# Two batches' heads in the opening of a fused attention and mixing kernel

## The chip, the cores and the metric

One core of a Trainium2 chip runs the kernel. The metric is device time in microseconds of that core. The time before is 978.15 us, the median of three runs (977.51 to 978.64).

## The reference, cut to what matters

```python
# q, k, v: (8, 8, 576, 64), float32
scores = 1 / sqrt(64) * q @ k.T
mask_local   = (rel >= 0) & (rel < 32)                       # heads 0..3, rel = i - j
mask_strided = (rel >= 0) & (j % 32 == i % 32)               # heads 4..7
attn = softmax(where(mask, scores, -1e9))
x = (attn @ v) as (8, 576, 512)
h = x^T @ U @ V                                              # along the sequence, rank 32
u = x + h^T
out = u + relu(u @ w_ch1) @ w_ch2                            # 512 -> 2048 -> 512
```

U, V, w_ch1 and w_ch2 arrive as float64. Every float32 product of the large GEMMs is made of three: high part by high part, high by low, low by high.

## The kernel before, in words

**Tiling.** The 8 x 576 rows are nine blocks of 512: block n < 8 holds the first 512 rows of batch n, block 8 the last 64 rows of all batches. For each block the two GEMMs run over 16 chunks of 128 hidden features (`fc`). A step is `gemm1(fc)` (12 matmuls 128x512, L616), a relu split into a high part `gh` on ScalarE (L620) and a low part `gl` on VectorE (L621), and `gemm2` of the chunk before (12 matmuls, L633). The GEMMs read u transposed, as `uh` and `ul`, which `split` makes from `raw` at a block's end (L607, L608).

**Weights.** A chunk of both weights is 1 MB of 64-bit words. `load_weights` brings it in on SP's queue, `weights` converts it: one ScalarE instruction (L122), three of VectorE (L124, L125, L127), a rounding on ScalarE (L173) and a difference on VectorE (L174). The buffer `cv` in which this is done is double and lies in the one "wide" buffer, which the strided heads need afterwards. `N_FIRST` chunks are converted ahead of the first step, in halves of 512 columns; the others one chunk a step in block 0, each made to follow in order the `gl` of the step `BEHIND` = 5 before it.

**Attention.** Heads come in pairs; below, "a head" is such a pair of 128 columns. The first `NSP` = 2 batches run local and strided heads alike through `early_pair`: `scores` (L301, L307), `probabilities` (max L316, difference L317, exp L321), `transposed` (L328, copy L331), `outputs` (PV, L341), `normalised` (L350, L351, L353, L357). Then comes the head's quarter of u^T: x is transposed on PE (L277) and multiplied with U (L238, L240), copied and split into `tst` (L245 to L247), and multiplied with V onto the same sums (L249); for batch 0 the result goes into `uh` and `ul` (L259, L260), for batch 1 into `raw` (L255). Strided heads of these batches are computed with rows sorted by class and go through DRAM (`od`) into natural order, on POOL's queue (L99). From batch 2 on, strided heads are element by element on POOL and VectorE (`strided_heads`, L400, L402, L428, L430), copied in place by ScalarE (L445, L449), and local heads go through PE.

**Order.** `first_attention` is the opening: all of batch 0's heads, staggered by one stage. Then `convert(2 * N_FIRST)`, then the steps. After each half step (a slot, 32 to a block) `advance` pulls items of the next batch's attention so that they are spread from slot `a0` to `a1` of the block; what is left at `a1` is drained there. In block 0 that is batch 1: tail of batch 0, then its four heads. In block 1 it is batch 2. Strided heads are spread separately, from slot 20 of block 0 on and not before all chunks are converted; where the attention of a batch says "strided" they are drained. A planner orders the instructions of each engine by its own cost model with this order as priority; `issue_after` adds an order on one engine.

**Buffers.** PSUM has two pairs of banks named acc, one px and two single banks ph. In the opening all three pairs rotate; in the steps acc belongs to gemm2 and px alone to attention. The tag "att" has five SBUF buffers for s_sb, PT, x, tmp, s_st and others; in the opening a ring of slices of weight buffers stands in for it. Weight buffers `w8` to `w15` hold batch 0's head data as `late`, `w7` is `early`. The tag "half" has three.

Of the kernel before, what the change touches and what calls it, by code (L numbers as in the profile page):

```python
# [7 lines left out]
F32 = mybir.dt.float32  # L8
F32R = mybir.dt.float32r
# [6 lines left out]
NEG = -1.0e9  # L16
ATT_BUFS = 5
NSP = 2
N_EARLY = 19
N_LATE = 48  # L20
N_STRIDED = 66
LAG = 1
LAGB = 3
CLA = 5
N_FIRST = 7
BEHIND = 5
A_EARLY = (1, 24, N_EARLY)
A_SECOND = (1, 28, 50)
A_LATE = (1, 28, N_LATE)
A_TAIL = (4, 20, 8)  # L30
S0 = {b: 32 * (b - 1) - 12 for b in range(2, 8)}
# [6 lines left out]
def fused_kernel(ctx, tc, pairs, strided, U, V, w_in, masks, eye, out):  # L38
# [21 lines left out]
    def att(shape, name, dtype=F32):  # L60
        if ring:
            s = ring.pop(0)
            ring.append(s)
            n = 1
            for x in shape[1:]:
                n *= x
            s = s[0:shape[0], 0:n]
            return s if len(shape) == 2 else s.rearrange("p (t h x) -> p t h x", t=shape[1], h=shape[2]) if len(shape) == 4 \
                else s.rearrange("p (t x) -> p t x", t=shape[1])
        return ap_.tile(shape, dtype, name=name, tag="att", bufs=ATT_BUFS)  # L70

    def half_buffer(width, name):
        return ap_.tile([128, 1176], F32, name=name, tag="half", bufs=3)[:, 0:width]
# [86 lines left out]
    def weights():  # L160
        cvs = wide_buffer("cv")
        for fc in range(NFC):
            load_ahead(fc + 1)
            cv = cvs[:, 1152 * (fc % 2):1152 * (fc % 2) + 1024]
            n = 512 if fc < N_FIRST else 1024
            with tc.issue_after(marks["gl"][fc - BEHIND]) if fc >= N_FIRST else nullcontext():
                for x in range(0, 1024, n):
                    to_f32(raws[fc][:, x:x + n], cv[:, x:x + n], 128, n)
            fv = cv.rearrange("p (i x) -> p i x", i=2)
            yield  # L170
            parts = w_parts[fc] = const.tile([128, 2, 2, 512], F32R, name=f"w{fc}", tag=f"w{fc}")
            for x in range(2) if fc < N_FIRST else [slice(0, 2)]:
                nc.scalar.copy(out=parts[:, x, 0], in_=fv[:, x])  # L173
                nc.vector.tensor_tensor(out=parts[:, x, 1], in0=fv[:, x], in1=parts[:, x, 0].bitcast(F32), op=ALU.subtract)  # L174
            yield
# [10 lines left out]
    halves = [slice(64 * hh, 64 * hh + 64) for hh in range(2)]  # L186

    def load_qk(b, pr):
        qk = late[2 * ORDER0.index(pr)][:, 0:2 * S] if b == 0 else half_buffer(2 * S, "qk")
        dma(out=qk, in_=pair_source(b, pr)[:, 0:2 * S])  # L190
        return qk[:, 0:S], qk[:, S:2 * S]

    def load_v(b, pr):
        vx = late[2 * ORDER0.index(pr) + 1][:, 0:PAIR - 2 * S] if b == 0 else half_buffer(PAIR - 2 * S, "v")
        dma(out=vx, in_=pair_source(b, pr)[:, 2 * S:PAIR])
        return vx.rearrange("p (c x) -> p c x", x=D + 1)

# [3 lines left out]
    def early_pair(b, pr, od, last):  # L201

        tb = 64 * (b % 2)
        by_class = pr >= 2
        kT, qT = load_qk(b, pr)
        yield
        if b == 0:
            vt = load_v(b, pr)
            yield
        with tc.issue_after(marks["PV"][3]) if b else nullcontext():  # L210
            sp = scores(kT, qT, mask_s if by_class else mask_l)
        s_sb = yield from probabilities(sp)
        if b:
            vt = load_v(b, pr)
        yield
        PT = transposed(s_sb)
        yield
        op = outputs(PT, vt)
        cs = slice(2 * pr * D, 2 * pr * D + 2 * D)
        if by_class:  # L220
            x = att([128, 640], "x").rearrange("p (t x) -> p t x", t=5) if b else \
                early[:, 320 + 640 * (pr - 2):960 + 640 * (pr - 2)].rearrange("p (t x) -> p t x", t=5)
            main, last_x, Um = x[:, 0:4, :], x[0:64, 4, :], U_c
            normalised(op, x)
        else:
            xg, xt = x_tiles(b)
            main, last_x, Um = xg[:, :, cs], xt[tb:tb + 64, cs], U_sb
            normalised(op, main, last_x, tb)
        p0 = 0 if by_class else tb
        yield  # L230
        pu = psx2().rearrange("p a x -> p (a x)")
        pm = ps_h.tile([128, 512], F32, name="ph")[0:32, 0:128] if b == 0 else pu[0:32, 640:768]
        lead = x_transposed(pu, [main[:, t, :] for t in range(4)])
        if by_class:
            lead = x_transposed(pu[:, 512:576], [last_x])
        with tc.issue_after(lead):
            for t in range(4):
                nc.tensor.matmul(pm, Um[:, t, :], main[:, t, :], start=t == 0 and not (b and by_class), stop=False,  # L238
                                 skip_group_check=True, tile_position=(0, 0))
            nc.tensor.matmul(pm, Um[p0:p0 + 64, 4, :], last_x, start=False, stop=True, skip_group_check=True,  # L240
                             tile_position=(p0, 0))
        if b not in tsts:
            tsts[b] = ap_.tile([96, DM], F32R, name="tst")
        tst = tsts[b]
        nc.scalar.copy(out=tst[0:32, cs], in_=pm)  # L245
        nc.scalar.copy(out=tst[64:96, cs], in_=pm)
        nc.vector.tensor_tensor(out=tst[32:64, cs], in0=pm, in1=tst[0:32, cs].bitcast(F32), op=ALU.subtract)  # L247
        for c0, n, Vm in ((0, 512, Vc), (512, 64, Vc_last)) if by_class else ((0, 512, Vst),):
            nc.tensor.matmul(pu[:, c0:c0 + n], tst[:, cs], Vm[:, 0:n], start=False, stop=True, skip_group_check=True)  # L249
        src = pu[:, 0:512]  # L250
        if by_class:
            src = pu[:, 0:S].rearrange("p (c j) -> p j c", j=NCH)[:, 0:16, :]
        if b:
            dst = raw[:, :, :, pr, :]
            nc.scalar.copy(out=dst, in_=src.rearrange("p (s a) x -> p s a x", s=4) if by_class else  # L255
                           src.rearrange("p (s a x) -> p s a x", s=4, a=4))
        else:
            hi, lo = (u[:, pr, :].rearrange("p (j c) -> p j c", c=32) if by_class else u[:, pr, :] for u in (uh, ul))
            one = nc.scalar.copy(out=hi, in_=src)  # L259
            two = nc.vector.tensor_tensor(out=lo, in0=src, in1=hi.bitcast(F32), op=ALU.subtract)  # L260
            marks["split0"] = (two.ins, one.ins)
        if by_class:
            oc = 2 * pr * D - 4 * D
            far_dma(out=od[0:512, oc:oc + 2 * D].rearrange("(t p) d -> p t d", p=128), in_=main)
            far_dma(out=od[512:576, oc:oc + 2 * D], in_=last_x)
        yield
        if last:
            od_reads(b, od)

    def x_transposed(pu, parts):  # L270

# [255 lines left out]
    def first_attention():  # L527
        tsts[0] = ap_.tile([96, DM], F32R, name="tst")
        sw = small_weights()
        next(sw)  # L530
        for x in range(8):
            late[x] = const.tile([128, 2048], F32, name="late", tag=f"w{NFC - 8 + x}")
            ring.append(late[x][:, 1176:1816])
        pairs0 = [early_pair(0, pr, ods[0], pr == ORDER0[3]) for pr in ORDER0]
        for pair in pairs0:
            next(pair)
            next(pair)
            if pair is pairs0[0]:
                dma(out=mask_s, in_=masks[:, 448:768])
                dma(out=masks_sb, in_=masks[:, 0:448])  # L540
                dma(out=ident, in_=eye)
        next(sw)
        load_ahead(1)
        next(pairs1[0])
        load_ahead(2)
        next(pairs1[1])
        load_ahead(NFC // 2 - 1)
        running = run_staggered(pairs0, LAG)
        for _ in range(2):
            next(running)  # L550
            yield
        next(sw)
        yield from running
        ring.clear()

    def attention(b):
        if b >= NSP:
            if b == NSP:
                yield from mix_tail(1)
            yield from local_pairs(b)  # L560
            yield from mix_t(b, 0)
            yield "strided"
# [6 lines left out]
        else:  # L569
            tail = mix_tail(0)  # L570
            next(tail)
            yield
            running = run_staggered(pairs1, LAGB)
            for _ in range(6):
                next(running)
                yield
            yield from tail
            yield from running

    pairs1 = [early_pair(1, pr, ods[1], pr == ORDER1[3]) for pr in ORDER1]  # L580

    def transposes(n):

# [66 lines left out]
            next(conv)  # L650
            counts["conv"] += 1

    for _ in first_attention():
        pass
    convert(2 * N_FIRST)
    banks["prefix"] = False

# [25 lines left out]
    def advance(slot):  # L683
# [2 lines left out]
        if k == 0 and n < B:  # L686
            gen, done = (attention(n + 1) if n + 1 < B else tail_block()), 0
        if gen is not None:
            a0, a1, total = A_EARLY if n == 0 else A_SECOND if n == 1 else A_LATE if n + 1 < B else A_TAIL
# [104 lines left out]
```

## Time and profile before

| | |
|---|---|
| median of 3 runs | 978.15 us |
| profiled execution's own time | 979.34 us |
| its span | 977.5 us |
| mean granted TensorE clock | 0.966 |
| PE / PEld busy | 919.1 / 733.2 us |
| DVE / ACT / POOL busy | 559.8 / 247.2 / 319.0 us |
| bytes moved by DMA | 74.24 MB |

The span is the part of the execution in which the engines have instructions; the execution's own time lies 1.84 us over it. Engines are PE (TensorE matmuls), PEld (its weight loads), DVE (VectorE), ACT (ScalarE), POOL (GpSimd), SP (the queue of DMA issues). L12 is line 12 of the kernel. Matmuls overlap in the pipeline, so their listed durations are longer than their spacing. "idle before <-releaser" says how long an engine stood still ahead of a group and what ended that.

### The profile page before, as it was taken

To read this page: it belongs to the slowest core of one execution; us is meant where nothing else is said; L and a number is where in the kernel's file an instruction comes from. 1 tells how busy PE (TensorE), PEld (TensorE's weight loads), DVE (VectorE), ACT (ScalarE), POOL (GpSimd) and SP (SyncE) were. 2 spreads that over 40 slices of the span, in tenths; PEclk is the share of its full clock that TensorE was granted. 3 is DMA by queue.
4 is the path that set the end of the run, shared out by engine and by line. 5 is a ranking of instruction groups with operands and counts; after the bars stand their busy time and mean duration, and the time that the engine had idled before them with its cause. 6 is when DMAs were issued, how large, how long until landed. Compare 5 with 4: busy or idle time off the path is not lost.

```text
span 977.5 us, 16779 instructions
## 1 busy us (share of the span) xinstructions
PE 919.1 (94%) x7032; PEld 733.2 (75%) x7032; DVE 559.8 (57%) x907; ACT 247.2 (25%) x485; POOL 319.0 (33%) x354
## 2 busy tenths in 40 slices
PE   4569999899976999999999999999999999999996
PEld 2457787687754778877787778777877888888885
DVE  4954684674777667865886588658765441122111
ACT  4632452211401241224122412241224111121110
POOL 0110020672475438443844394339433000000000
PEclk9679999899996999999999999999999999999998
DMA  9951222210024010501150105011500131001001
GB/s 367 422 206 50 80 62 99 93 61 1 1 76 169 13 49 24 191 7 49 28 181 3 49 25 195 2 50 32 177 1 2 40 107 36 1 1 44 1 1 43
DMA packets 35772, 74.24 MB, mean 76 GB/s; under 512 B 5840, under 2 KB 20560, under 8 KB 32880
## 3 DMA queue, kind: packets, MB, share of 16 engines
q1 hardware_dynamic: 25776, 67.13, 19.3%
q10 hardware_dynamic: 8960, 3.68, 1.5%
q0 software_dynamic: 960, 2.36, 0.8%
q8 instruction: 55, 0.90, 0.4%
q14 instruction: 21, 0.17, 0.1%
HBM read 54.14 MB, written 11.67 MB: 67 GB/s over the span
## 4 chain that ended last, share of the span: by engine, by line
PE 86%; DVE 7%; DMA 2%; POOL 2%; ACT 1%; issue 1%; SPq 0%; DVEq 0%; ACTq 0%; POOLq 0%
PE ph L616 39%; PE acc L633 39%; POOL tmp L400 2%; PE px L341 2%; PE px L307 1%; DMA w<-in_w_dram 1%; PE px L328 1%; DVE st L430 1%; DVE cv L125 1%; DVE w L174 1%; DVE cv L127 1%; PE px L471 1%; DMA late<-in_pairs_dram 1%; DMA st<-in_strided_dram 1%; PE px L494 0%
## 5 line engine op out<-in xcount | busy, mean ns | idle before, releaser
L616 PE MATMUL ph<-uh,w 128*128 128x512 f32 x1152 | 385.3, 395 | 0.2 <-ACT uh L607 0.2
L633 PE MATMUL acc<-w,gh 128*128 128x512 f32 x1152 | 355.7, 394 | 4.6 <-ACT gh L620 4.6
L633 PEld LDWEIGHTS acc<-w,gh 128*128 128x128 f32 x1152 | 216.4, 189 | 50.9 <-ACT gh L620 5.1
L616 PEld LDWEIGHTS ph<-uh,w 128*128 128x128 f32 x1152 | 217.5, 190 | 47.3 <-issue 0.6
L621 DVE SCALAR_TENSOR_TENSOR gl<-ph,gh 128x512 fp32r<-128x512 f32 x144 | 99.0, 688 | 242.8 <-ACT gh L620 242.2
L616 PE MATMUL ph<-ul,w 128*128 128x512 f32 x576 | 227.6, 395 | 0.5 <-DVE ul L608 0.5
L633 PE MATMUL acc<-w,gl 128*128 128x512 f32 x576 | 221.7, 395 | 5.0 <-DVE gl L621 5.0
L620 ACT ACTIVATE gh<-ph 128x512 fp32r<-128x512 f32 x144 | 85.9, 597 | 468.6 <-PE ph L616 378.5
L400 POOL TENSOR_TENSOR tmp<-st 128x576 f32<-128x576 f32 (+6 forms) x162 | 167.4, 1070 | 104.8 <-DMA st<-in_strided_dram 57.2
L428 POOL TENSOR_TENSOR tmp<-st,s_st 128x448 f32<-128x448 f32 (+7 forms) x162 | 136.5, 871 | 181.6 <-DVE st L430 96.2
L430 DVE TENSOR_REDUCE st<-tmp 128x64 f32<-128x64 f32 (+8 forms) x162 | 137.1, 879 | 14.8 <-POOL tmp L428 13.9
L633 PEld LDWEIGHTS acc<-w,gl 128*128 128x128 f32 x576 | 108.7, 189 | 29.6 <-DVE gl L621 5.9
L616 PEld LDWEIGHTS ph<-ul,w 128*128 128x128 f32 x576 | 109.2, 190 | 24.3 <-DVE ul L608 0.9
L402 DVE TENSOR_REDUCE s_st<-tmp 128x9 f32<-128x576 f32 (+6 forms) x162 | 87.4, 563 | 23.3 <-POOL tmp L400 22.2
L445 ACT COPY xg<-st 32x256 f32<-32x256 f32 x96 | 38.7, 404 | 8.0 <-DVE st L430 6.7
L482 DVE TENSOR_TENSOR ta<-px,ta 32x256 f32<-32x256 f32 x36 | 15.1, 420 | 35.3 <-ACT ta L480 34.5
L639 DVE TENSOR_TENSOR xg<-acc,xg 128x512 f32<-128x512 f32 x36 | 22.9, 681 | 9.4 <-PE acc L633 9.4
L99 POOL DMA_DIRECT2D od<-x x4 | 2.8, 708 | 77.8 <-DVE x L353 77.8
L122 ACT ACTIVATE cv<-w 128x512 f32<-128x512 f32 (+1 forms) x23 | 19.3, 855 | 23.6 <-DMA w<-in_w_dram 11.5
L321 ACT ACTIVATE s_sb<-s_sb 128x640 f32<-128x640 f32 x16 | 11.8, 740 | 51.4 <-DVE s_sb L317 51.4
L608 DVE TENSOR_TENSOR ul<-raw,uh 128x512 fp32r<-128x512 f32 x32 | 21.4, 691 | 5.9 <-ACT uh L607 5.9
L316 DVE TENSOR_REDUCE mx<-px 128x10 f32<-128x640 f32 x16 | 13.1, 821 | 18.7 <-PE px L307 18.7
(140 smaller groups left out, 514.8 us busy)
## 6 DMA issues: line engine op xcount, KB each, us to landing
w<-in_w_dram SPq DMA_DIRECT2D x16, 1024.0 KB, 15.9
v<-in_pairs_dram SPq DMA_DIRECT2D x16, 585.0 KB, 5.2
qk<-in_pairs_dram SPq DMA_DIRECT2D x16, 576.0 KB, 5.1
out_dram<-xg SPq DMA_DIRECT2D x32, 256.0 KB, 2.0
st<-in_strided_dram SPq DMA_DIRECT2D x6, 1152.0 KB, 5.5
raw<-bt SPq DMA_DIRECT2D x112, 32.0 KB, 1.9
raw<-bt ACTq DMA_DIRECT2D x112, 32.0 KB, 1.9
st<-in_strided_dram SPq DMA_DIRECT2D x6, 576.0 KB, 4.1
```

The source lines that it names most:

```text
L341: last = nc.tensor.matmul(op[32 * o4:32 * o4 + 32, hh, (D + 1) * t:(D + 1) * t + D + 1], PT[rows, 32 * c:32 * c + 32], vt[rows, c], start= ...
L400: nc.gpsimd.tensor_tensor(out=tmp[:, 0:n], in0=sk[:, j0:j0 + n], in1=sq[:, i:i + 1].broadcast_to([128, n, D]), op=ALU.mult)
L402: late.append(lambda tmp=tmp, n=n, i=i, j0=j0: nc.vector.tensor_reduce(out=s_st[:, i, j0:j0 + n], in_=tmp[:, 0:n], axis=AX.X, op=ALU.add))
L428: nc.gpsimd.tensor_tensor(out=tv, in0=sv[:, 0:i + 1, d0:d0 + step], in1=s_st[:, i, 0:i + 1].broadcast_to([128, i + 1, step]), op=ALU.mult)
L430: late.append(lambda tv=tv, i=i, d0=d0, step=step: nc.vector.tensor_reduce(out=o_st[:, i, d0:d0 + step], in_=tv.rearrange("p j d -> p d j" ...
L445: nc.scalar.copy(out=xg[32 * i4:32 * i4 + 32, :, cs], in_=o_st[rows, i4:16:4, :])
L608: nc.vector.tensor_tensor(out=lo, in0=raw[:, :, :, dc, :], in1=hi.bitcast(F32), op=ALU.subtract)
L616: nc.tensor.matmul(ph, w_parts[fc][:, 0, part, 128 * dc:128 * dc + 128], ut[:, dc, :], start=(dc == dcs[0] and i == 0), stop=(dc == dcs[-1 ...
L620: nc.scalar.activation(out=gh, in_=ph, func=AF.Relu)
L621: low = nc.vector.scalar_tensor_tensor(out=gl, in0=ph, scalar=0.0, in1=gh.bitcast(F32), op0=ALU.max, op1=ALU.subtract)
L633: nc.tensor.matmul(accs[n][s // 2][:, s % 2, :], gt[:, cs], w_parts[fc][:, 1, part, :], start=(fc == 0 and i == 0 and n >= NSP), stop=(fc ...
L639: nc.vector.tensor_tensor(out=ot, in0=accs[n][s // 2][:, s % 2, :], in1=ot, op=ALU.add)
```

## The change

- `first_attention` runs the heads of both batches, eight in all, staggered by one stage. `early_pair` ends with the head's x, its write to `od` and, for the last head, the reads of `od`. What follows is a function of its own, `quarter`. For batch 0 it is called as the pair's last stage; for batch 1 in block 0's slots.
- All eight heads' q, k and v are loaded first: masks, head 0, identity, head 1, U and V, heads 2 to 5, the first weight chunk, heads 6 and 7, then weights 1 to 6. q and k of batch 0 lie in the buffers of `w2` to `w5`, of batch 1 in `w6` and the three "half" buffers; v of all eight in `late`.
- Five chunks, not seven, are converted ahead of the steps. The first chunk's conversion follows in ScalarE's order the sixth head's exp, the other four the eighth's.
- In block 0 there remain: batch 0's tail, four quarters, batch 1's tail (nine items, slots 2 to 24). In block 1 batch 1's tail is gone, and the pace is that of the later blocks.
- x of batch 1's class-sorted heads and its `tst` lie in "att".

```diff
-N_EARLY = 19
+N_EARLY = 9
-LAGB = 3
-N_FIRST = 7
+N_FIRST = 5
-A_EARLY = (1, 24, N_EARLY)
-A_SECOND = (1, 28, 50)
+A_EARLY = (2, 24, N_EARLY)
...
-            with tc.issue_after(marks["gl"][fc - BEHIND]) if fc >= N_FIRST else nullcontext():
+            with tc.issue_after(marks["gl"][fc - BEHIND] if fc >= N_FIRST else marks["exp"][7 if fc else 5]):
...
     def load_qk(b, pr):
-        qk = late[2 * ORDER0.index(pr)][:, 0:2 * S] if b == 0 else half_buffer(2 * S, "qk")
+        place = NFC // 2 - 6 + 4 * b + ORDER0.index(pr)
+        if b < NSP and place < NFC // 2 - 1:
+            qk = const.tile([128, 2 * S], F32, name="qk", tag=f"w{place}")
+        else:
+            qk = half_buffer(2 * S, "qk")
...
-        vx = late[2 * ORDER0.index(pr) + 1][:, 0:PAIR - 2 * S] if b == 0 else half_buffer(PAIR - 2 * S, "v")
+        vx = late[4 * b + ORDER0.index(pr)][:, 0:PAIR - 2 * S] if b < NSP else half_buffer(PAIR - 2 * S, "v")
...
         kT, qT = load_qk(b, pr)
-        yield
-        if b == 0:
-            vt = load_v(b, pr)
-            yield
-        with tc.issue_after(marks["PV"][3]) if b else nullcontext():
-            sp = scores(kT, qT, mask_s if by_class else mask_l)
+        vt = load_v(b, pr)
+        yield
+        sp = scores(kT, qT, mask_s if by_class else mask_l)
...
+        parts[b, pr] = (main, last_x, p0)
+        if last:
+            od_reads(b, od)
+        yield
+        if b == 0:
+            quarter(b, pr)
+            yield
+
+    def quarter(b, pr):
+
+        main, last_x, p0 = parts[b, pr]
...
-            tsts[b] = ap_.tile([96, DM], F32R, name="tst")
+            tsts[b] = ap_.tile([96, DM], F32R, name="tst", **({"tag": "att", "bufs": ATT_BUFS} if b else {}))
...
+        heads = [early_pair(b, pr, ods[b], pr == ORDER0[3]) for b in range(NSP) for pr in ORDER0]
+        dma(out=mask_s, in_=masks[:, 448:768])
+        dma(out=masks_sb, in_=masks[:, 0:448])
+        for k, pair in enumerate(heads):
             next(pair)
+            if k == 0:
                 dma(out=ident, in_=eye)
+            if k == 1:
+                next(sw)
+            if k == 5:
+                load_ahead(1)
+        running = run_staggered(heads, LAG)
+        next(running)
+        next(running)
         next(sw)
+        next(running)
+        next(sw)
+        for _ in running:
+            pass
+        ring.clear()
         load_ahead(NFC // 2 - 1)
...
-            if b == NSP:
-                yield from mix_tail(1)
...
-            running = run_staggered(pairs1, LAGB)
-            for _ in range(6):
-                next(running)
+            for pr in ORDER1:
+                quarter(b, pr)
                 yield
             yield from tail
-            yield from running
+            yield from mix_tail(1)
```

More of the change, by code (lines that the diff above doesn't have):

```diff
@@ L70, in att, with att5 @@
         return ap_.tile(shape, dtype, name=name, tag="att", bufs=ATT_BUFS)
+    def att5(shape, name):
+        return ap_.tile(shape, F32, name=name, tag="att", bufs=ATT_BUFS)
     def half_buffer(width, name):
@@ L205, in early_pair @@
         kT, qT = load_qk(b, pr)
+        vt = load_v(b, pr)
         yield
-        if b == 0:
-            vt = load_v(b, pr)
-            yield
-        with tc.issue_after(marks["PV"][3]) if b else nullcontext():
-            sp = scores(kT, qT, mask_s if by_class else mask_l)
+        sp = scores(kT, qT, mask_s if by_class else mask_l)
         s_sb = yield from probabilities(sp)
-        if b:
-            vt = load_v(b, pr)
         yield
@@ L220, in early_pair @@
         if by_class:
-            x = att([128, 640], "x").rearrange("p (t x) -> p t x", t=5) if b else \
+            x = att5([128, 640], "x").rearrange("p (t x) -> p t x", t=5) if b else \
                 early[:, 320 + 640 * (pr - 2):960 + 640 * (pr - 2)].rearrange("p (t x) -> p t x", t=5)
-            main, last_x, Um = x[:, 0:4, :], x[0:64, 4, :], U_c
+            main, last_x, p0 = x[:, 0:4, :], x[0:64, 4, :], 0
             normalised(op, x)
@@ L226, in early_pair @@
             xg, xt = x_tiles(b)
-            main, last_x, Um = xg[:, :, cs], xt[tb:tb + 64, cs], U_sb
+            main, last_x, p0 = xg[:, :, cs], xt[tb:tb + 64, cs], tb
             normalised(op, main, last_x, tb)
-        p0 = 0 if by_class else tb
-        yield
+        if by_class:
+            oc = 2 * pr * D - 4 * D
+            far_dma(out=od[0:512, oc:oc + 2 * D].rearrange("(t p) d -> p t d", p=128), in_=main)
+            far_dma(out=od[512:576, oc:oc + 2 * D], in_=last_x)
+        parts[b, pr] = (main, last_x, p0)
+        if last:
+            od_reads(b, od)
+        yield
+        if b == 0:
[3 more added lines that the diff above has]
+        main, last_x, p0 = parts[b, pr]
+        by_class = pr >= 2
+        cs = slice(2 * pr * D, 2 * pr * D + 2 * D)
+        Um = U_c if by_class else U_sb
         pu = psx2().rearrange("p a x -> p (a x)")
@@ L261, in early_pair @@
             marks["split0"] = (two.ins, one.ins)
[L262 to L265, printed above, removed]
-        yield
-        if last:
-            od_reads(b, od)
+    parts = {}
     def x_transposed(pu, parts):
@@ L529, in first_attention @@
         sw = small_weights()
-        next(sw)
         for x in range(8):
@@ L533, in first_attention @@
             ring.append(late[x][:, 1176:1816])
-        pairs0 = [early_pair(0, pr, ods[0], pr == ORDER0[3]) for pr in ORDER0]
-        for pair in pairs0:
+        heads = [early_pair(b, pr, ods[b], pr == ORDER0[3]) for b in range(NSP) for pr in ORDER0]
+        dma(out=mask_s, in_=masks[:, 448:768])
+        dma(out=masks_sb, in_=masks[:, 0:448])
+        for k, pair in enumerate(heads):
             next(pair)
[L537 to L540, printed above, removed]
+            if k == 0:
                 dma(out=ident, in_=eye)
-        next(sw)
[L543 to L546, printed above, removed]
-        load_ahead(NFC // 2 - 1)
-        running = run_staggered(pairs0, LAG)
-        for _ in range(2):
-            next(running)
-            yield
-        next(sw)
-        yield from running
-        ring.clear()
+            if k == 1:
[5 more added lines that the diff above has]
+        next(running)
+        next(sw)
+        next(running)
[3 more added lines that the diff above has]
+        ring.clear()
+        load_ahead(NFC // 2 - 1)
     def attention(b):
         if b >= NSP:
-            if b == NSP:
-                yield from mix_tail(1)
             yield from local_pairs(b)
@@ L572, in attention @@
             yield
-            running = run_staggered(pairs1, LAGB)
-            for _ in range(6):
-                next(running)
+            for pr in ORDER1:
+                quarter(b, pr)
                 yield
             yield from tail
-            yield from running
-    pairs1 = [early_pair(1, pr, ods[1], pr == ORDER1[3]) for pr in ORDER1]
+            yield from mix_tail(1)
     def transposes(n):
@@ L651, in convert @@
             counts["conv"] += 1
-    for _ in first_attention():
-        pass
+    first_attention()
     convert(2 * N_FIRST)
@@ L688, in advance @@
         if gen is not None:
-            a0, a1, total = A_EARLY if n == 0 else A_SECOND if n == 1 else A_LATE if n + 1 < B else A_TAIL
+            a0, a1, total = A_EARLY if n == 0 else A_LATE if n + 1 < B else A_TAIL
             want = 10 ** 6 if k >= a1 else total * (k + 1 - a0) // (a1 - a0)
```

## The prediction, made before the change was run

> **What bounds the kernel now.** I read the page first, then the second relu of each block, then the busy time by stretches, then the chain of waits around the two places that stood out. The page's first row says that TensorE is busy nearly always:
>
> ```profile
> PE 919.1 (94%) x7032; PEld 733.2 (75%) x7032; DVE 559.8 (57%) x907; ACT 247.2 (25%) x485; POOL 319.0 (33%) x354
> ```
>
> That is an average over stages with different limits. The second gh of a block (L620, ScalarE, second matmul step) is a fixed point from which the second GEMM runs; ScalarE's timeline gives it for blocks 0, 1, 2 and 3 (start us, duration):
>
> ```profile
> 74.10 0.60 ACT L620 ACTIVATE gh<-ph 128x512 fp32r<-128x512 f32 x1 [1.23 <-PE ph L616]
> ...
> 196.45 0.60 ACT L620 ACTIVATE gh<-ph 128x512 fp32r<-128x512 f32 x1 [1.24 <-PE ph L616]
> ...
> 314.43 0.60 ACT L620 ACTIVATE gh<-ph 128x512 fp32r<-128x512 f32 x1 [0.48 <-PE ph L616]
> ...
> 411.73 0.60 ACT L620 ACTIVATE gh<-ph 128x512 fp32r<-128x512 f32 x1 [2.35 <-PE ph L616]
> ```
>
> So the opening takes 74.1 us, block 0 122.35, block 1 117.98 and block 2 97.30. From 314.4 to the end are 977.5 - 314.4 = 663.1 us, which I leave as they are. Stretches (start:end, length, then busy us of PE, PEld, DVE, ACT, POOL, the granted clock, DMA share, GB/s):
>
> ```profile
> 9.00:21.00 12.00, 10.18 (x350) 6.58 (x349) 5.70 (x7) 4.37 (x10) 0.00 (x0) 0.86 1.02 421
> 21.00:57.00 36.00, 18.15 (x263) 14.52 (x264) 35.20 (x70) 20.40 (x37) 6.63 (x10) 0.68 1.01 403
> 72.00:180.00 108.00, 106.11 (x991) 84.41 (x989) 63.05 (x80) 36.98 (x52) 7.21 (x13) 1.00 0.25 81
> 250.00:308.00 58.00, 43.26 (x198) 32.89 (x191) 45.03 (x74) 16.67 (x41) 38.65 (x40) 0.84 0.23 73
> 308.00:405.00 97.00, 97.00 (x735) 77.43 (x734) 67.45 (x112) 25.40 (x55) 50.56 (x54) 0.99 0.20 67
> ```
>
> The opening is VectorE's (35.20 of 36) while PE works half the time; block 0 is PE's (106.11 of 108); at the end of block 1 PE is idle for 58.00 - 43.26 = 14.7 us; block 2 is full. What PE waits for in block 1 begins in block 0. POOL's timeline of strided(2), and the first strided copies of batches 2 and 3 on ScalarE, with the last weight conversion on VectorE:
>
> ```profile
> 159.88 0.32 POOL L400 TENSOR_TENSOR tmp<-st 128x64 f32<-128x64 f32 x1 [19.74 <-PE px L328]
> 166.07 0.46 POOL L400 TENSOR_TENSOR tmp<-st 128x128 f32<-128x128 f32 x1 [5.87 <-PE px L341]
> 180.54 27.73 POOL L400 TENSOR_TENSOR tmp<-st 128x192 f32<-128x192 f32 x25 [14.02 <-PE px L328]
> ```
> ```profile
> 259.89 1.23 ACT L445 COPY xg<-st 32x256 f32<-32x256 f32 x3 [0.24 <-DVE st L430]
> ...
> 350.53 1.65 ACT L445 COPY xg<-st 32x256 f32<-32x256 f32 x4 [1.10 <-DVE st L430]
> ```
> ```profile
> 150.27 1.23 DVE L174 TENSOR_TENSOR w<-cv,w 128x1024 fp32r<-128x1024 f32 x1 [0.24 <-ACT w L173]
> ```
>
> Conversion ends at 151.5, yet POOL gets going only at 180.54: its products and the heads' s_sb and PT share five buffers of one tag, and it sits behind PE's reads of them. Its copies come at 259.89, 63.4 us into block 1, against 350.53 - 314.43 = 36.1 us into block 2, which shows no hole.
>
> **The change, part by part.** *(a) Four heads leave block 0.* A head there costs PE, by the chain of waits (start, length, what):
>
> ```profile
> 100.18 0.29 PE px L301 x2
> 100.47 0.85 PE px L307 x48
> ...
> 121.06 0.65 PE px L328 x5
> ...
> 122.42 1.04 PE px L341 x64
> ```
>
> That is 2.83 us, 11.3 for four. Four quarters of the second batch stay, each
>
> ```profile
> 107.67 1.25 PE px L277 x10
> 108.92 0.99 PE px L238 x8
> 109.91 0.33 PE px L240 x2
> ...
> 115.45 0.26 PE px L249 x2
> ...
> 131.88 2.72 PE ph L616 x12
> ```
>
> again 2.83 us, 11.3 in all. The last row is half a step of GEMM: 16 steps x 2 x 2.72 = 87.0 us a block. Before, 87.0 + 11.3 + 11.3 = 109.6, and the other 12.7 us of block 0's 122.35 are holes, chiefly at its end, where the last two heads are forced out one after the other. After: 87.0 + 11.3 + 1 for the tails + 2 for the change of blocks = 101.4 (bounds 99 and 110, the holes halved). Block 0 then carries 11 conversions in place of 9, each 4 to 5 us of VectorE (below) beside one gl (0.69 by the page's 99.0 / 144):
>
> ```profile
> L621 DVE SCALAR_TENSOR_TENSOR gl<-ph,gh 128x512 fp32r<-128x512 f32 x144 | 99.0, 688 | 242.8 <-ACT gh L620 242.2
> ```
>
> 5.6 us against a step of 5.44 plus its share of the quarters, 0.7: covered by PE, just, and five chunks are done ahead. Without that cover the two extra conversions would show as 10 us.
>
> *(b) The opening gets four heads, loses two conversions, and conversions queue behind the heads' exps on ScalarE.* VectorE's groups of the opening (count, busy us, mean ns):
>
> ```profile
> L174 DVE TENSOR_TENSOR w<-cv,w 128x512 fp32r<-128x512 f32 x14 | 9.3, 684 | 0.7 <-ACT w L173 0.7
> L125 DVE SCALAR_TENSOR_TENSOR cv<-w,cv 128x512 int32<-128x512 int32 x14 | 9.2, 683 | 0.0
> L127 DVE SCALAR_TENSOR_TENSOR cv<-w,cv 128x512 int32<-128x512 int32 x14 | 9.2, 684 | 0.0
> L124 DVE TENSOR_SCALAR cv<-cv 128x512 int32<-128x512 int32 x14 | 5.5, 422 | 3.1 <-ACT cv L122 3.0
> L316 DVE TENSOR_REDUCE mx<-acc 128x10 f32<-128x640 f32 x4 | 3.3, 823 | 3.7 <-PE acc L307 3.7
> L317 DVE TENSOR_TENSOR late<-acc,mx 128x640 f32<-128x640 f32 x4 | 3.3, 823 | 0.1
> L260 DVE TENSOR_TENSOR ul<-acc,uh 128x512 fp32r<-128x512 f32 x4 | 2.7, 674 | 3.0 <-ACT uh L259 3.0
> ```
>
> A conversion is 2 x (0.684 + 0.683 + 0.684 + 0.422) = 4.95 us, a head 0.82 + 0.82 + 0.82 (L353, below) and some 0.3 of small ones = 2.8, a quarter about 1. Scores start at 8.88:
>
> ```profile
> 8.88 0.71 PE L301 MATMUL acc<-early,masks_sb 128*128 128x320 bf16 x2 [8.88 <-DMA masks_sb<-in_masks_dram]
> ```
>
> so 8.88 + 8 x 2.8 + 4 x 1 + 5 x 4.95 = 60.0 if VectorE never rests. It rested 12.0 - 5.7 = 6.3 us in 9:21, before the weights came. With that the second gh, call it X, is at 67. Low bound: the planner lets the first gl pass the chunks that are not yet needed, X = 50 (60.0 less two of the conversions). High bound: waiting for exp costs a whole set of four conversions at the end, with nothing to fill the heads' gaps, X = 85 (the four heads ran to 62, four more on PE alone 11, four conversions less overlap 12).
>
> The eight loads of the second batch go ahead of most weights on SP's queue, the two batches together 9.3 MB by the page's sizes:
>
> ```profile
> w<-in_w_dram SPq DMA_DIRECT2D x16, 1024.0 KB, 15.9
> v<-in_pairs_dram SPq DMA_DIRECT2D x16, 585.0 KB, 5.2
> qk<-in_pairs_dram SPq DMA_DIRECT2D x16, 576.0 KB, 5.1
> ```
>
> With five weight chunks that is 14.5 MB, 35 us at the 403 to 421 GB/s above, so all are there by 38, before VectorE gets to them: hidden. w2 to w7 now sit on SP behind the release of head buffers; those go free in the heads' own order, by 50. The second batch's writes and reads of od move into the opening too, on POOL's queue, where POOL was busy for 6.63 of 36 us with the first batch's and nothing else waits.
>
> *(c) strided(2) starts when conversion ends.* The last chunk may follow gl number 10, at X + 54.4 + 11.3 + 2, and takes 4.95, so it ends near X + 72.6 = 139.6; its load, at 5.5 by the last row of the page, gives POOL's start at 145.1, where it was 180.54: 35.4 earlier.
>
> ```profile
> st<-in_strided_dram SPq DMA_DIRECT2D x6, 1152.0 KB, 5.5
> ```
>
> From there the chain that ended block 1 is unchanged, 79.4 us to the copies and 54.5 more to block 2. So block 2's second gh comes at 314.4 - 35.4 = 279.0. PE alone would get there at 67 + 101.4 + 97.3 = 265.7; the chain is later, and I take it.
>
> **Sum.** 279.0 + 663.1 = 942.1 us of span, 35.4 less. The profiled execution's own time is 979.34, so 943.9; the median is 978.15, 1.2 below that execution, so 942.8.
>
> [...] In 21:57 the granted clock is 0.68 with PE half busy, in 72:180 it is 1.00. PE's work in the new opening is 12 x 2.83 = 34.0 us at full clock, which fits ahead of X; at half clock it is 68, and X would be 8.88 + 68 + 2.72 = 79.6, a result of its own (second rival). [...]
>
> **The rivals.** *The chain of block 1 does not bind.* With the heads gone from the five buffers POOL may run through its second half faster than in 79.4 us; then PE sets block 2's start at 265.7, and the total is 265.7 + 663.1 = 928.8 of span, 930 against the median. For it: POOL's waits above are PE's; against: the same chain in block 2 took as long while PE was full.
>
> *The opening is PE's, at half clock.* X = 79.6, POOL's start 157.7, gain 22.8, time 955. For it: 0.68; against: conversions no longer stretch the heads' cycle, so PE idles less.
>
> *Slower: eight heads in series.* In the opening before, norm followed norm at (61.75 - 25.23) / 3 = 12.2 us over four heads:
>
> ```profile
> 25.23 0.82 DVE L353 TENSOR_TENSOR early<-acc,rt 128x640 f32<-128x640 f32 x1
> ...
> 61.75 0.69 DVE L353 TENSOR_TENSOR xg<-px,rt 128x512 f32<-128x512 f32 x1
> ```
>
> If the rotation of three PSUM pairs keeps that pace for eight, the last norm is at 25.2 + 7 x 12.2 = 110.6, the gated conversions end 15 later (they overlap the last head), X = 124, and the time is 124 + 875 (72.6 + 5.5 + 79.4 + 54.5 + 663.1) = 999. It decides from X = 102.4, where POOL's start is back at 180.54. Against it: half of these gaps were filled with conversion that VectorE had to do anyway, and only four of the eight have a quarter.
>
> *The change does not do what it says.* The planner orders by its own clock; it may set the second batch's PV and softmax behind the first steps. Then 11.3 us return to block 0 and POOL's buffers stay held; only the holes at the end of block 0 go: some 10 us, 968.
>
> **How the numbers follow.** Forecast 0.57 (its own range 925 to 958), chain gone 0.18, half clock 0.12, series 0.06, order unchanged 0.07. What this kernel can tell from no change is about 0.2%, 2 us. Faster holds the first three and most of the last, 0.91; the slower case with a margin 0.07; within 0.2% 0.02. The range runs from the low bound of X with no chain, 50 + 101.4 + 97.3 + 663.1 = 912, to the last rival's side, 964; outside lie the series case and the tails.
>
> **What would show it.** Second gh of block 0 at 60 to 75 (right), beyond 80 (the opening step is wrong). Block 0 from second gh to second gh near 101, without L301, L307 or L341 of the second batch in it. POOL's first long run of L400 near 145, directly after the last L174. If the hole at the end of block 1 shrinks from 14.7 us to a few, the first rival; if it stays, the chain. Blocks 2 to 8 at 97.3 and 87 as before; a change there, or an end of conversion that PE waits for in block 0, would make the prediction wrong.

## The result, and the profile after

The kernel after takes 953.33 us (median of four runs, 952.53 to 954.16) against 978.39 us before on the same chip: a ratio of 0.9743, 95% interval 0.9726 to 0.9760, or 25.1 us less. Forecast were 943 us and a range of 912 to 964. The profiled execution has a span of 952.4 us and a time of 954.16 us. The page's first row:

```profile
PE 916.7 (96%) x7032; PEld 733.6 (77%) x7032; DVE 561.2 (59%) x899; ACT 245.7 (26%) x481; POOL 318.1 (33%) x354
```

The second gh of blocks 0 to 3 on ScalarE's timeline (now L625), which cuts the kernel into the terms of the prediction:

```profile
78.55 0.60 ACT L625 ACTIVATE gh<-ph 128x512 fp32r<-128x512 f32 x1 [0.26 <-PE ph L621]
...
180.58 0.60 ACT L625 ACTIVATE gh<-ph 128x512 fp32r<-128x512 f32 x1 [3.73 <-PE ph L621]
...
289.47 0.60 ACT L625 ACTIVATE gh<-ph 128x512 fp32r<-128x512 f32 x1 [0.99 <-PE ph L621]
...
386.77 0.60 ACT L625 ACTIVATE gh<-ph 128x512 fp32r<-128x512 f32 x1 [2.35 <-PE ph L621]
```

| stretch, us | before | predicted | after |
|---|---|---|---|
| opening, to the second gh (X) | 74.1 | 67 | 78.6 |
| block 0 | 122.4 | 101.4 | 102.0 |
| block 1 | 118.0 | 110.6 | 108.9 |
| block 2 and the rest | 663.1 | 663.1 | 662.9 |

(The last is 952.4 - 289.5.) Both blocks came out within 2 us of the sum; the opening became 4.5 us longer, where 7 us less were forecast. Stretches of the kernel after (length, busy us of PE, PEld, DVE, ACT, POOL, clock, DMA share, GB/s):

```profile
21.00:57.00 36.00, 28.76 (x679) 22.15 (x680) 18.02 (x37) 10.75 (x23) 5.76 (x10) 0.93 1.02 395
...
78.50:180.60 102.10, 102.02 (x493) 82.26 (x499) 84.39 (x109) 42.64 (x61) 24.59 (x26) 1.00 0.08 26
180.60:289.50 108.90, 102.96 (x757) 81.05 (x761) 78.44 (x133) 25.77 (x57) 60.30 (x67) 0.95 0.22 74
```

In block 0 PE is busy for 102.02 of 102.10 us: its idle time is gone. In block 1 PE is idle for 5.9 us, and it is busy for 102.96 us at a granted clock of 0.95 where block 2 takes 97.3 in all. In 21:57 VectorE, busy for 35.20 us before, is busy for 18.02, and four of the conversions that it used to do there wait for the eighth exp (ScalarE, the first exp, the eighth, and the conversion behind it):

```profile
9.11 0.74 ACT L332 ACTIVATE late<-late 128x640 f32<-128x640 f32 x1 [7.09 <-DVE late L328]
...
64.76 0.74 ACT L332 ACTIVATE late<-late 128x640 f32<-128x640 f32 x1 [5.49 <-DVE late L328]
65.40 0.64 ACT L123 ACTIVATE cv<-w 128x512 f32<-128x512 f32 x1
```

PE's clock in the opening is lower than the 0.93 of that row suggests. From 44 us to the second gh, 16.6 of 34.6 us were granted at half:

```profile
44.00:78.55 34.55, 25.97 (x533) 19.10 (x534) 24.77 (x52) 15.07 (x27) 6.30 (x11) 0.76 1.01 387
```

And the trace has no record of the clock before 27.9 us, which the row counts as full. Ten transposes of a head took 2.69 us at 22.83 and 1.52 at 32.37, so PE most likely ran slow there too:

```profile
22.83 2.69 PE L288 MATMUL acc<-ident,early 128*128 128x128 f32 x10
...
32.37 1.52 PE L288 MATMUL px<-ident,early 128*128 128x128 f32 x10
```

So VectorE does not bound the new opening, though its sum gave the forecast of X. What does is the subject of the experiments. None of them leaves anything out of the computation. Times are medians, ratios are to the kernel before on the same chip; the kernel before came out at 977.96 to 980.75 us from group to group of runs, so runs of different groups are compared by ratio. Times of single events are from one profile each. One execution, of the first run of experiment 3, took 3126.81 us for a reason that stays open, and the ratio of that run goes by its other three.

### The profile page after: what moved, and what is told of

Same layout as the page of the kernel before. It is cut to its first block, busy times and chain, and to the rows that moved or that the text cites. A ratio compares the mean times of both kernels' runs of the same rounds, so it can differ in the third digit from the quotient of the medians.

```text
span 952.4 us, 16775 instructions
## 1 busy us (share of the span) xinstructions
PE 916.7 (96%) x7032; PEld 733.6 (77%) x7032; DVE 561.2 (59%) x899; ACT 245.7 (26%) x481; POOL 318.1 (33%) x354
## 2 busy tenths in 40 slices
DMA packets 35772, 74.24 MB, mean 78 GB/s; under 512 B 5840, under 2 KB 20560, under 8 KB 32880
## 4 chain that ended last, share of the span: by engine, by line
PE 86%; DVE 5%; POOL 3%; DMA 2%; issue 2%; ACT 1%; SPq 0%; DVEq 0%; ACTq 0%; POOLq 0%
PE ph L621 39%; PE acc L638 38%; POOL tmp L411 3%; PE px L352 1%; DMA st<-in_strided_dram 1%; PE px L318 1%; DVE st L441 1%; PE px L339 1%; DMA xg<-in_U_dram 1%; PE px L482 1%; PE px L288 1%; PE ph L254 1%; PE acc L288 1%; PE px L505 1%; DVE ul L613 0%
## 5 line engine op out<-in xcount | busy, mean ns | idle before, releaser
L625 ACT ACTIVATE gh<-ph 128x512 fp32r<-128x512 f32 x144 | 86.0, 597 | 479.6 <-PE ph L621 388.9
L613 DVE TENSOR_TENSOR ul<-raw,uh 128x512 fp32r<-128x512 f32 x32 | 24.8, 797 | 2.7 <-ACT uh L612 2.7
L507 DVE TENSOR_TENSOR xg<-px,xg 128x512 f32<-128x512 f32 x24 | 15.4, 685 | 11.8 <-PE px L505 11.8
L175 DVE TENSOR_TENSOR w<-cv,w 128x1024 fp32r<-128x1024 f32 (+1 forms) x21 | 20.0, 966 | 3.8 <-ACT w L174 3.8
L123 ACT ACTIVATE cv<-w 128x1024 f32<-128x1024 f32 (+1 forms) x21 | 18.8, 925 | 11.1 <-DVE w L175 11.0
L592 DVE STREAM_TRANSPOSE bt<-xg 128x512 f32<-128x512 f32 x28 | 19.2, 698 | 2.0 <-DMA xg<-ud 2.0
```

The lines of the kernel that those rows point to most:

```text
L613: nc.vector.tensor_tensor(out=lo, in0=raw[:, :, :, dc, :], in1=hi.bitcast(F32), op=ALU.subtract)
L625: nc.scalar.activation(out=gh, in_=ph, func=AF.Relu)
```

## The experiments

**1. The order behind the exps.** Two edits of the line that holds the early conversions back:

```diff
-marks["exp"][7 if fc else 5]
+marks["exp"][5]                       # first run
...
+marks["gl"][fc - BEHIND]) if fc >= N_FIRST else nullcontext()   # second run: no order
```

> Base: the kernel after, 953.3 us, second gh of block 0 at 78.6, last conversion ends at 147.3. One edit: all five early conversions follow the sixth head's exp, not the eighth's. Theory 'gate' (VectorE stands idle in the opening because the conversions are held behind the eighth exp): they fill VectorE's gaps between 45 and 65, second gh at 68 to 72, last conversion near 140, block 2 earlier by the same, total 944 to 948. Rival 'heads' (PE and the rotation of PSUM pairs set the opening; conversions among the heads only stretch them): eighth exp later than 64.8, second gh 77 to 82, total 952 to 957.

> The kernel after without any order between the early conversions and the exps. Theory 'gate': VectorE is filled as in the kernel before (over 90% from 21 to 57), its sum of 60 us plus some idle time at the start sets second gh at about 67, total about 942. Rival 'heads': the heads are stretched to the 12 us cycle seen before, the eighth exp comes at 75 or later, second gh at 80 to 95, total 955 to 970.

Behind the sixth exp: 948.74 us, ratio 0.9695 (0.9675 to 0.9714). Second gh at 71.7, as 'gate' had it, last conversion at 143.5, and yet the eighth exp slipped from 64.8 to 67.9, as 'heads' had it; block 0 took 104.3 instead of 102.0, which gave 2.3 of the 6.8 us back. With no order: 951.32, ratio 0.9728 (0.9710 to 0.9747), second gh at 72.2, eighth exp at 69.3, and VectorE still short of full:

```profile
21.00:57.00 36.00, 24.53 (x611) 18.76 (x610) 28.36 (x56) 17.91 (x34) 6.43 (x10) 0.87 1.01 391
```

Neither theory as stated. The order behind the eighth exp costs 4.7 us by the ratios against the order behind the sixth; without any order the gain, 1.5 us, lies within the intervals. In neither run does X come down to 67, and the eight heads take somewhat longer than in the kernel after. Something else paces them.

**2. The quarters behind all heads.** To see whether the fourth quarter's PSUM pair holds up the eighth head:

```diff
         if b == 0:
+            for _ in range(4):
+                yield
             quarter(b, pr)
             yield
```

> The kernel after, but each quarter of batch 0 is taken four stages later, behind the scores of all eight heads. Theory 'PSUM' (the eighth head's scores start at 61 because the pair they need is held by the fourth quarter until 60): eighth exp before 52, conversions from there, second gh at 70 to 74 if the quarters fit beside the conversions, total 945 to 949. Rival 'PE order' (the eighth scores stand at 61 because gemm1 and the waits on PE are ahead of them): eighth exp still at 58 or later, and the quarters come on top, second gh beyond 80, total 955 to 962.

962.85 us, ratio 0.9842 (0.9826 to 0.9858); eighth exp at 57.5, second gh at 88.8. With no quarter among them the heads still needed until 57.5, which is more than 'PSUM' allows, and the quarters then came on top. PE's waits in 21:57 of this run (line, releaser, us in total, times, longest) say why:

```profile
PE acc L320 <- issue: 9.1, 4, 3.7
PE acc L354 <- issue: 5.6, 2, 3.9
```

"issue" is time in which PE waits for nothing that the profile shows: 14.7 us in 36, in the middle of the scores and of PV, and for no data. In the kernel after such breaks stand on PE's timeline:

```profile
47.30 0.88 PE L318 MATMUL acc<-qk 64*32 64x64 f32 x66 [1.75 <-issue]
...
54.87 0.76 PE L352 MATMUL px<-late 64*32 64x65 f32 x37 [2.20 <-issue]
...
74.54 0.40 PE L514 MATMUL px<-tst,Vst 96*64 96x512 f32 x1 [2.39 <-issue]
```

Counted over all of PE's records (matmuls, weight loads and its few others), the breaks come at these places, and on the trace's instruction queue (q8) 16 KB blocks start at these times:

```
kernel after, breaks of PE over 0.6 us by "issue": at record 449, 705, 1729, 1985, 2753   (each 193 + a multiple of 256)
quarters last:                                     at record 449, 705, 961, 1217, 1473, 1729, 1985
kernel after, 16 KB blocks start at us: 13.5 19.6 26.0 32.3 38.5 44.8 52.2 58.2 65.3 72.3 80.1 98.8
kernel before:                          14.1 20.1 29.8 44.6 57.0 67.3 80.1 93.8
```

The breaks lie a whole number of 256 records apart. While data keep the DMA engines full (share about 1.02), the blocks of the kernel after start 5.9 to 7.8 us apart, and from one of these places to the next PE takes no less than 5.8 us. A head's scores and PV are 72 + 80 matmuls with a weight load each, and the second gh comes some 2800 records in: nearly eleven blocks, or 67 us by an estimate at 6.2 us a block. The kernel before spread half of the heads over block 0. Its first two blocks came 6.0 us apart, and PE broke off there for 3.4 us; after them its blocks came 9.7 us apart or more up to 93.8, and "issue" stopped PE for 0.5 us more in all.

The page of the kernel after counts the packets of the instruction queue, their MB and their share of 16 engines' time:

```profile
q8 instruction: 55, 0.90, 0.4%
```

Each of the 55 has 16384 bytes in the trace. PE's records are 14130 (7032 matmuls, 7032 weight loads, 66 others), so 257 to a packet, which agrees with the spacing of the breaks.

**3. Emptier DMA engines.** If that is the limit, weights that nobody needs yet should be kept from the queues. A transfer of 256 bytes from a head's x, ahead of the chunks on SP's queue, does it:

```diff
+            with tc.issue_after(marks["hold"]) if fc >= 5 else nullcontext():
                 dma(out=raws[fc], in_=w_in[128 * fc:128 * fc + 128, :])
...
+        load_ahead(5)
+        marks["hold"] = nc.sync.dma_start(out=held, in_=parts[1, 3][0][0:1, 0, 0:64]).ins
         load_ahead(NFC // 2 - 1)
```

The other three runs of this group change the first chunk that is held (1 or 3), the head (`parts[0, 1]`, `parts[1, 2]`), and in two of them the order to `exp[5]` as in experiment 1.

> The kernel after, but weight chunks 5 to 15 are not fetched before the sixth head's x is written (a 256-byte transfer from x stands ahead of them on SP's queue). Nothing is left out. In the kernel after PE's rows in the opening break off at instructions 705, 1729 and 1985, a whole number of 256 apart, and one 16 KB block on the instruction queue starts every 6.2 us while the DMA engines are full. Theory 'fetch' (PE's supply of instructions paces the heads while data fill the DMA engines): with the engines idle between about 38 and 60 the blocks come faster there, the eighth exp moves from 64.8 to 54 to 59, second gh of block 0 from 78.6 to 69 to 74, total 945 to 950. Rival 'PE' (the heads' matmuls and the PSUM rotation pace it, fetch is only seen where PE waits anyway): eighth exp 63 to 66, total 952 to 956.

> The kernel after, but weight chunks 1 to 15 are not fetched before the fourth head's x is written, so that the DMA engines are idle from about 30 to 40. Theory 'fetch': blocks on the instruction queue closer than 4 us apart in that stretch, 6 us again once the weights move; eighth exp at 55 to 60. The weights themselves are there by 55, before conversion needs them: second gh 68 to 74, total 944 to 950. Rival 'PE': eighth exp 63 to 66, total 952 to 957 with the weights later.

> Chunks 5 to 15 held as in the run before last, and the early conversions behind the sixth exp instead of the eighth. By 'fetch' the two gains add, since one frees PE and the other fills VectorE: second gh 64 to 70, last conversion near 138, total 941 to 946. By 'PE' only the 4.6 us of the earlier conversions remain: 947 to 950.

> Chunks 3 to 15 held behind the fifth head's x, early conversions behind the sixth exp. By 'fetch' as the run before, with the DMA engines idle from about 33: second gh 63 to 70, total 940 to 947; the weights must not become late, chunk 3 is needed some 15 us after its release. By 'PE' 947 to 951.

| held | order behind | us | ratio (95%) | eighth exp | second gh | last conversion |
|---|---|---|---|---|---|---|
| none (kernel after) | exps 6, 8 | 953.33 | 0.9743 (0.9726 to 0.9760) | 64.8 | 78.6 | 147.3 |
| 5 to 15 | exps 6, 8 | 946.87 | 0.9653 (0.9637 to 0.9669) | 56.8 | 71.9 | 140.8 |
| 1 to 15 | exps 6, 8 | 947.28 | 0.9664 (0.9640 to 0.9689) | 56.7 | 73.0 | 141.4 |
| 5 to 15 | exp 6 | 944.22 | 0.9626 (0.9611 to 0.9641) | 63.1 | 67.0 | 140.6 |
| 3 to 15 | exp 6 | 948.51 | 0.9670 (0.9655 to 0.9684) | 62.3 | 70.3 | 143.8 |

In the first run every engine has the same instructions in the same order as in the kernel after, and only the weights move at another time; the eighth exp comes 8 us earlier: 'fetch'. The gain lies between the sixth exp (44.0 us in both) and the eighth:

```profile
44.00:64.76 20.76, 16.71 (x352) 12.18 (x353) 11.43 (x23) 5.87 (x12) 1.82 (x3) 0.75 1.01 371
```
```profile
44.00:56.80 12.80, 12.08 (x352) 9.30 (x353) 11.25 (x23) 5.80 (x11) 1.34 (x2) 1.00 0.59 146
```

The same 352 matmuls: PE's idle time falls from 4.1 us to 0.7, and its busy time from 16.7 to 12.1, because the clock is 1.00 there instead of 0.75. In the kernel after it drops to half at 48.3 and 55.2, each time close behind a break (the two end at 47.30 and 54.87), and with the breaks gone so are these drops. (Not every break has one: behind that at 56.33 in the second run the clock stays full, 1.00 in 50:60.) The first six exps did not move, in the second run either, although its blocks came as close as 3.6 us from 32 us on: between 32 and 44 us the supply of instructions does not set the pace. The stretch 40:57 of the kernel after, and then of the first of these runs:

```profile
40.00:57.00 17.00, 12.51 (x345) 9.27 (x343) 10.60 (x22) 5.74 (x12) 3.23 (x6) 0.85 1.02 367
```
```profile
40.00:57.00 17.00, 15.85 (x516) 11.97 (x514) 13.37 (x27) 7.09 (x15) 4.58 (x8) 1.00 0.69 188
```

With the DMA share at 0.69 PE gets through 516 matmuls in the 17 us, not 345. The blocks there start at 38.6, 43.0, 47.1 and 51.4, so 4.1 to 4.4 us apart; with chunks 1 to 15 held, 32.3 and 35.9. When its weights move again, that second run has breaks at records 2241 and 2497, which the kernel after doesn't have. The share was still 1.01 in 38.6:43.0, so it is not the share itself that spaces the blocks; what does was not measured. The fourth run fell into the rival's band, for the reason that its expectation names: its weights are late. ScalarE stands still for 2.95 us until 66.00, when a held chunk lands, and between 50 and 100 PE waits for a converted chunk:

```profile
PE ph L626 <- ACT w L175: 4.9, 2, 2.7
```

1.0 us is the same wait in the third run. That third run, 944.22, is the best version found: 1.2% faster than the kernel after by the ratios, 9 us by the medians.

**4. Seven chunks first.** The kernel after with `N_FIRST = 7`, as before the change.

> The kernel after with seven chunks converted ahead of the first step, as before the change, and all else as in it. By the prediction's sum (VectorE sets the opening) two conversions more cost 2 x 4.95 us there: second gh at 85 to 88, and nothing is saved behind it but VectorE's load in block 0: total 955 to 963. By 'gate and fetch' (the opening waits for the eighth exp and the second chunk alone, the rest follows beside the steps) second gh stays at 77 to 80, total 951 to 956.

953.27 us, ratio 0.9732 (0.9714 to 0.9750), second gh at 77.9: no difference to the kernel after, as 'gate and fetch' had it. VectorE's sum of the opening, on which two conversions more would be 10 us, is not what PE waits for.

**5. What ends block 1.** Four runs. First, in the kernel after, strided(2) eight slots later in the order; then, on the base of the best version, its load in two halves into the conversion's buffer; conversion seven steps ahead; and, on top of the latter, strided(2) six slots earlier.

```diff
-S0 = {b: 32 * (b - 1) - 12 for b in range(2, 8)}
+S0 = {b: 32 * (b - 1) - (12 if b > 2 else 4) for b in range(2, 8)}    # first; the last has 18 for 4
...
-        st = wide_buffer("st")
-        dma(out=st, in_=strided[b - NSP, :, 0:2 * NCH * D])
+        st = wide["cv"] if b == NSP else wide_buffer("st")
+        for x in range(2):
+            dma(out=st[:, x * NCH * D:(x + 1) * NCH * D], in_=strided[b - NSP, :, x * NCH * D:(x + 1) * NCH * D])
...
-N_FIRST = 5
-BEHIND = 5
-CLA = 5
+N_FIRST = 7
+BEHIND = 7
+CLA = 7
```

> The kernel after, but the strided heads of batch 2 may start eight slots (four steps) later in block 0. Theory 'chain' (start of strided(2) plus 80 us plus 55 us is the start of block 2): POOL's long run starts at 164 to 168, not 154, the hole in block 1 grows from 11 us by as much, total 962 to 968. Rival 'PE' (block 1 is bound by something else at its end, as split or the planner's order): hole unchanged, total 952 to 955.

> The best kernel so far (chunks 5 to 15 held, early conversions behind the sixth exp; 944.2) with one edit: the strided data of batch 2 go into the conversion's own buffer in two transfers, so that the half which the last chunk does not use is loaded while that chunk is converted. Theory 'chain' (end of conversion, load, POOL, copies, block 2): POOL's long run starts 3 to 4 us after the last conversion, not 5.9, and the total falls by 2 to 3, 941 to 942.5. Rival 'PE or VectorE ends block 1': POOL starts earlier, total unchanged within 1, 943.5 to 945.

> The same base with conversion up to seven steps ahead of the steps instead of five (and seven chunks before the first). Theory 'chain': where VectorE has room the last conversion ends one to two steps earlier (129 to 136, not 140.6), block 2 earlier by the same: 934 to 941. Rival 'VectorE is full in block 0' (60 of 67 us busy between 80 and 147 in the kernel after): last conversion not before 138, and gl comes late behind conversions, total 943 to 950.

> Conversion seven steps ahead, as in the run before (944.15; block 1 takes 107.9 us from second gh to second gh), and the strided heads of batch 2 may start six slots earlier in the order (eight slots later had made block 1 5.5 us longer). Theory 'order' (block 1's hole depends on how many of strided(2)'s items stand ahead of block 1 in the order, not on when POOL starts): block 1 at 102 to 105, total 939 to 942. Rival 'POOL start' (POOL cannot begin before the last conversion and the load, 144, so items placed earlier only wait): block 1 as before or VectorE waits at the end of block 0, total 943 to 948.

| run | us | ratio (95%) | last conversion | POOL starts strided(2) | first copies | block 1 | POOL starts strided(3), after block 1's second gh | from there to block 2 |
|---|---|---|---|---|---|---|---|---|
| before | 978.39 | 1 | 151.5 | 159.9, in a row 180.5 | 255.4 | 118.0 | 77.3 | 40.7 |
| after | 953.33 | 0.9743 | 147.3 | 154.1 | 229.2 | 108.9 | 67.7 | 41.2 |
| 8 slots later | 959.86 | 0.9811 (0.9794 to 0.9827) | 146.6 | 152.2 | 232.3 | 114.4 | 71.3 | 43.0 |
| best version | 944.22 | 0.9626 (0.9611 to 0.9641) | 140.6 | 146.5 | 220.8 | 108.1 | 67.7 | 40.4 |
| load in halves | 944.12 | 0.9639 (0.9623 to 0.9655) | 139.9 | 144.4 | 218.9 | 108.5 | 67.6 | 40.9 |
| 7 ahead | 944.15 | 0.9636 (0.9619 to 0.9652) | 138.4 | 144.1 | 219.9 | 107.9 | 67.3 | 40.7 |
| 6 slots earlier | 947.42 | 0.9676 (0.9654 to 0.9698) | 137.2 | 142.8 | 211.4 | 110.7 | 68.3 | 42.4 |

Eight slots later did not delay POOL's start (152.2 for 154.1), against both theories, and still made block 1 5.5 us longer. The halves and the longer lead did bring POOL's start forward by 2.1 and 2.4 us, and block 2 came no earlier: the rivals' result in both. In the last run the first four copies came 8.5 us earlier, the next ones 1.6, and block 1 was 2.8 us longer, where 'order' had it at 102 to 105. By these runs block 1's end hangs neither on POOL's start nor on the first copies alone, though the steps of 2 us are small. What the rows share is the start of the next batch's strided heads. POOL's row in the kernel before, and in the kernel after:

```profile
273.78 11.23 POOL L400 TENSOR_TENSOR tmp<-st 128x64 f32<-128x64 f32 x13 [8.33 <-DMA st<-in_strided_dram]
```
```profile
248.32 27.53 POOL L411 TENSOR_TENSOR tmp<-st 128x64 f32<-128x64 f32 x27 [8.34 <-DMA st<-in_strided_dram]
```

They wait for the load of batch 3's data into the wide buffer, which batch 2's last copies release, and from here it is 40.4 to 43.0 us to block 2 in all fourteen kernels, the one before included. In this time VectorE's queue holds the reductions of POOL's 27 products ahead of the gl that gemm2 needs. The chain of waits of the kernel after runs through them:

```profile
242.84 5.35 DMA st<-in_strided_dram
...
251.31 18.11 POOL tmp L411 x17
269.44 0.75 DVE s_st L413
270.20 0.61 DVE gl L626
...
270.85 3.78 PE acc L638 x8
```

From 248 to 290, VectorE's and PE's longest waits are:

```profile
DVE s_st L413 <- POOL tmp L411: 8.4, 10, 3.1
```
```profile
PE px L312 <- DVE xt L520: 3.2, 1, 3.2
PE acc L638 <- DVE gl L626: 1.9, 1, 1.9
```

That strided(3) starts 67.3 to 68.8 us into block 1 in the twelve kernels other than the one before and the one with eight slots later points to the instruction order, which puts strided(2)'s last reductions among block 1's own steps. No run changes that place alone, so this is not shown, and the one run that moved strided(2) forward in the order lost 2.8 us, for a reason that stays open.

## Why the prediction was right or wrong

- **Block 0 (part a) was right in its total**, 102.0 for 101.4, but one term was misread. The 12.7 us called holes were idle time only in part: PE was busy for 118.46 of block 0's 122.35 us before, so idle for 3.9.

```profile
74.10:196.45 122.35, 118.46 (x1109) 92.89 (x1109) 73.32 (x102) 39.47 (x58) 23.12 (x29) 0.97 0.24 77
```

  Of the 20.3 us that left block 0, 3.8 were idle time and 16.5 PE's: 11.3 by the four heads, and the rest in part by the clock (0.97, now 1.00), which the sum has no term for. VectorE at 84.39 of 102.10 us carried the two extra conversions under PE, as the sum of 5.6 us a step against 6.1 had it.
- **The opening (part b) is the step that failed**: the term "60 us of VectorE plus 6.3 at rest, X = 67". It measured 78.6, between the two signs that the prediction names (60 to 75, beyond 80), and these 11.6 us are nearly the whole miss of the total. VectorE was taken as the bound because it was full before; the order behind the exps leaves it half idle. What PE was given in exchange, eight heads of small matmuls, is held up by instructions that arrive late while weights fill the DMA engines (share 1.01 in 44:64.76, with breaks of 1.75 and 2.20 us), and by the clock that drops behind some of the breaks (0.75 in that stretch). The sum has no term for either, and calls the loads "hidden". A row for it was in the profile before, among PE's waits of the opening, and the prediction does not use it:

```profile
PE acc L307 <- issue: 3.4, 2, 2.1
```

  In the run with chunks 5 to 15 held and the order behind exp 6, X is 67.0, the forecast's number. That is a coincidence, since neither obstacle was in the forecast.
- **The bounds held**: X lay between 50 and 85, the time between 912 and 964. They were wide; the range of 52 us had room for a miss of X by 11.6.
- **Strided(2) (part c): right in size, wrong in its link.** POOL's long run began at 154.07, directly after the last conversion, which is this row, and the load; the heads no longer held its buffers:

```profile
146.07 1.23 DVE L175 TENSOR_TENSOR w<-cv,w 128x1024 fp32r<-128x1024 f32 x1 [1.17 <-ACT w L174]
...
154.07 16.43 POOL L411 TENSOR_TENSOR tmp<-st 128x64 f32<-128x64 f32 x18 [74.28 <-DMA st<-in_strided_dram]
```

  From there to block 2 are 135.4 us, where 133.9 were taken. But the chain is not rigid from POOL's start on: experiment 5 moved the start by 2 us and the first copies by up to 8.5, and block 2 came no earlier. So that the sum came out so close is in part luck. Block 1 got 9.1 us shorter while strided(3) starts 67.7 instead of 77.3 us into it; that the one makes the other is argued, not shown. The copies at 259.89 and 350.53 that the prediction calls the first are not: those of batch 2 began at 255.40 and those of batch 3 at 339.84. The sum does not change by it, as its two parts meet at that point.
- **The rivals.** "Half clock" gave X = 79.6 and 955 us, nearer to the measurement than the forecast, and is right in part: PE and its clock, at half for 16.6 of the last 34.6 us, hold up the opening. Half was granted before the change too, 0.50 in 24:30 and in 38:47 of that profile. But it took all of PE's work at half clock and no idle time, and the breaks are not in it, so its number is luck as well. "Chain gone" had block 1 at 97.3; it took 108.9, near the chain's 110.6. PE's idle time in block 1 did shrink, from 14.7 us to 5.9, which by the prediction's own sign leans to this rival: the case lies between the two. "Series" fell at the pace of 12.2 us a head: the first and the eighth exp, 9.11 and 64.76, are 8.0 us a head apart; that the heads rather than VectorE decide the opening was right in it. (Its X of 124 should be 125.6 by its own terms.) "Order unchanged" fell: of the second batch's heads nothing but one normalisation on VectorE is left behind the second gh.
- **The clock** stood in the forecast only as that rival, with a chance of 0.12, and it did hold up the eight heads. It was higher than before (0.93 against 0.68 in 21:57), but 0.75 between the sixth and the eighth exp, and 1.00 there with the weights held: 4.6 of the 8.0 us gained are PE's busy time, 3.3 its idle time.

Of the 11.6 us by which X missed, 6.6 came back when the weights were held, and 4.9 more when the conversions were also let in behind the sixth exp. That order alone gave 6.8.

## What to carry to other kernels

Moving work into a stretch where an engine looks idle also moves its instructions there: count them, and see whether the DMA engines are full there. Here it was some 2800 records of PE, in blocks of 256, at a share of about 1.02. The sign was "issue" among the waits, in the middle of a run of small matmuls: breaks of 1.75 and 2.20 us. The weights that were not needed yet were not free while the DMA engines were full; holding them back by one transfer of 256 bytes gained more here (ratio 0.9653 against 0.9743) than either order of the conversions that was tried. Read the clock in stretches of a few microseconds: a mean over 21:57, 0.93, hid that it was at half for 16.6 of the last 34.6 us of the opening. And a chain whose parts add up to the right number has still to be broken once before it is believed: two runs that moved its start left its end in place.

## What the runs showed of the hardware

PE's instructions came in blocks of 16 KB in these runs: 55 blocks for 14130 records, and breaks that lie a multiple of 256 records apart. The page counts the blocks among its 35772 DMA packets. In the kernel after a block started every 5.9 to 7.8 us in the opening, where the engines' share was about 1.02; with weights held back, as often as every 3.6 to 4.4 us. GEMM steps need far fewer: 24 matmuls and their weight loads last 5.44 us, which makes 29.0 us for 256 records, and the last seven blocks of the kernel after start 28.7 to 29.2 us apart. With 152 matmuls to a head, late blocks held up the last two heads of the opening by 8.0 us. Less than half of that, 3.3 us, was PE standing still; the rest was its clock, which was granted at half behind two breaks of 1.75 and 2.20 us and in full, 1.00, when they were gone.
